# Reordering the first batch of a fused attention and MLP kernel, and handing one rearrangement to GpSimd

## The chip, the cores and the metric

The kernel runs on one core of one Trainium2 chip. The core has a matrix engine (TensorE, "PE" in the profile), three engines for elementwise work (VectorE "DVE", ScalarE "ACT" and GpSimd "POOL"), and a queue engine (SyncE, "SP") that only issues transfers here. Each engine runs its own instructions strictly in order, and waits on semaphores for the results of others. The metric is the device time of one execution in microseconds (us), as the median of several runs.

## The reference, cut to what matters

```
# q, k, v: (8, 12, 448, 64); w_in: (768, 2048); w_out: (2048, 768); alpha: (2048,)
scores = (1/8) * q @ k^T                       # per batch and head, 448 x 448
attn   = relu(scores) ** 2 / 448
x      = (attn @ v), heads side by side        # (3584, 768)
h      = x @ w_in
g      = max(h, 0) + alpha * min(h, 0)
out    = g @ w_out                             # (3584, 768), float32
```

Eight batches of twelve heads go through attention; then all 3584 tokens go through two matrix products with a leaky relu, whose slope is given per column, between them.

## The kernel before, in words

**Tiles.** Heads are taken four at a time. Such a group is called a quad; a batch has three (`NG = 3`), so there are 24, numbered `n = 0..23`, and batch 0 is quads 0, 1 and 2. The 448 positions of a sequence are split as 64 x 7, and the seven residues `j = 0..6` are the "chunks" of a quad. All matrix inputs are bf16; q, k, v and the weights are cast on the way in by transfers that GpSimd issues (`load_qk`, `load_v`, `load_w_in`, `load_w_out`). At most eight of these are in flight: each issue waits for the landing of the one eight places before it. For quad 0 alone, q and half of k come in as float32 by other queues (L129) and are cast on the chip (L138 to L140).

**Attention of a quad.** First q and k are turned, so that the head dimension lies on the partitions. There are two ways: `turn_pe` (L149) transposes on TensorE and copies the result out of PSUM into a tile `T`; `turn_dma` (L161) has VectorE rearrange q and k into a tile `perm` by two copies (L164), and then a transposing transfer on SyncE's queue writes `T`. Quads 0 to 4 are turned on TensorE, the rest by transfer. For each chunk, `score_mm` (L173) makes four matmuls into a pair of PSUM banks, `relu` (L184) takes them out as bf16 into one of seven `rl` buffers, on ScalarE (L187) or VectorE (L189), and `square` (L192) squares that into one of twelve `at` buffers. `attnv` (L200), called A@V here, multiplies the seven squared chunks with v in 28 matmuls, and two copies scale the result into `xT` (L215 to L218).

**The MLP.** `f1` (L254) makes six matmuls for one block of 128 hidden columns (`km` = 0, 1 need quad 0 of the batch, 2, 3 quad 1, and 4, 5 quad 2), and `f1_out` applies the leaky relu with one ScalarE and one VectorE instruction (L249, L250) into `gT`. Two batches share a `gT`; `f2` (L259) multiplies it with w_out, whose columns are held in two parts, the first third and the rest.

**What sets the order.** `tc.manual_schedule()` is on, so each engine's order is that of the program text. The text is a long list written out by hand: `sc(...)` makes scores and relus for given chunks and puts them on the list `late`; `sq(k)` squares the oldest `k` of that list; loads and turns stand between them. PSUM banks are given out by `take_bank`, `take_pair` and `hold` to whoever asks, the least recently taken first, and a taker waits until the earlier user's result has been read out. `some_early` lets f1 of batch 0 start on `km` 0 to 3 of its first four blocks, in four banks that are held, before A@V of quad 2 is done. From batch 1 on, attention chunks of the next batch are spread between f1 and f2.

**Around the change.** Batch 0 has no earlier work to fill TensorE with, so its chunks follow each other through score, relu and square. In front of quad 5's chunks stands a gate: `landed` (L376), a GpSimd copy of one element of quad 5's `T`, which holds back all loads behind it in GpSimd's queue until the transposing transfer of quad 5 has landed.

Of the kernel before, what the change touches and what calls it, by code (L numbers as in the profile page):

```python
# [13 lines left out]
ALU = mybir.AluOpType  # L14

PP = 64
NJ = 7
# [3 lines left out]
def kernel(  # L21
# [10 lines left out]
    nc = tc.nc  # L32
    B, H, S, D = q.shape
# [27 lines left out]
    alpha_sb = singles.tile([128, KF], F32)  # L61
    beta_sb = singles.tile([128, KF], F32)
    landed = singles.tile([1, 1], BF16)
# [28 lines left out]
    raw, vraw = {}, {}  # L92

    def load_qk(n, names="qk"):
        b, g = divmod(n, NG)
        for name in names:
            src = q if name == "q" else k
            t = raw_pool.tile([128, 2, NJ, D], BF16, tag=name, name=f"{name}raw")
            flat = src[b].rearrange("(m two) (pp j) d -> (two pp) m (j d)", two=2, j=NJ)
            nc.gpsimd.dma_start(out=t.rearrange("p m j d -> p m (j d)"), in_=flat[:, 2 * g:2 * g + 2])  # L100
            raw[(n, name)] = t

    def load_v(n):
        b, g = divmod(n, NG)
        t = v_pool.tile([128, 2, NJ, D], BF16, tag="v", name="vraw")
        flat = v[b].rearrange("(m two) (pp j) d -> (two pp) m (j d)", two=2, j=NJ)
        nc.gpsimd.dma_start(out=t.rearrange("p m j d -> p m (j d)"), in_=flat[:, 2 * g:2 * g + 2])  # L107
        vraw[n] = t
# [4 lines left out]
    def load_w_in(i):  # L113
        lo, hi = 512 * i, 512 * i + 512
        for hf in range(2):
            for e in range(2):
                nc.gpsimd.dma_start(out=w_in_sb[64 * hf:64 * hf + 64, :, e, lo:hi],  # L117
                                    in_=w_in_v[hf, e, :, :, lo:hi])

    def load_w_out(h, lo=0, hi=KF, step=4):  # L120
        for lo in range(lo, hi, step):
            nc.gpsimd.dma_start(out=w_out_sb[h][:, lo:lo + step], in_=w_out_v[:, lo:lo + step, COLS[h][0]:COLS[h][1]])

    FIRST = 4
    first, flat0 = {}, {}
# [9 lines left out]
    warm = psum[:, 7, :128]  # L135
    for _ in range(36):
        nc.tensor.matmul(warm, ident, ident, start=True, stop=True)
    for name, lo, hi, copy in (("q", 0, 4, nc.vector.tensor_copy), ("q", 4, NJ, nc.scalar.copy),  # L138
                               ("k", 0, 2, nc.vector.tensor_copy), ("k", 2, FIRST, nc.scalar.copy)):
        copy(raw[(0, name)][:, :, lo:hi].rearrange("p m j d -> p m (j d)"), first[name][:, :, D * lo:D * hi])  # L140
    load_qk(1)
    load_v(0)
    load_qk(2)
# [3 lines left out]
    T = {}  # L147

    def turn_pe(n, parts=(("q", 0, NJ, "D"), ("k", 0, NJ, "D"))):  # L149
        if n not in T:  # L150
            T[n] = T_pool.tile([128, 2, NJ, 128], BF16, tag="T", name="T")
        for name, lo, hi, eng in parts:
            ps = take_bank().bitcast(BF16)
            for j in range(lo, hi):
                for s in range(2):
                    nc.tensor.transpose(ps[64 * s:64 * s + 64, 128 * j:128 * j + 128], raw[(n, name)][:, s, j], ident)  # L156
            dst = T[n][:, "qk".index(name), lo:hi].rearrange("p j c -> p (j c)")
            copy = nc.vector.tensor_copy if eng == "D" else nc.scalar.copy
            copy(dst, ps[:, 128 * lo:128 * hi])  # L159

    def turn_dma(n):  # L161
        p = perm_pool.tile([128, 2, NJ, 2, D], BF16, tag="perm", name="perm")
        for i, name in enumerate("qk"):
            nc.vector.tensor_copy(p[:, i], raw.pop((n, name)).rearrange("p s j d -> p j s d"))  # L164
        t = T_pool.tile([128, 2, NJ, 128], BF16, tag="T", name="T")
        nc.sync.dma_start_transpose(out=t.rearrange("p a j c -> p (a j) c"),
                                    in_=p.rearrange("p a j s d -> p (a j s d)"))
        T[n] = t
# [23 lines left out]
    def square(n, j, rl, eng="D"):  # L192
        a = at_pool.tile([128, 2, S], BF16, tag="at", name="at")
        if eng == "A":
            nc.scalar.activation(a, rl, ACTF.Square)
        else:
            nc.vector.tensor_tensor(a, rl, rl, ALU.mult)  # L197
        att[(n, j)] = a

    def attnv(n):  # L200
        ps = take_pair()
        vv = vraw.pop(n)
        for j in range(NJ):
            a = att.pop((n, j))
            for r in range(2):
                for s in range(2):
                    nc.tensor.matmul(ps[64 * s:64 * s + 64, r, :S],  # L207
                                     vv[64 * r:64 * r + 64, s, j, :],
                                     a[64 * r:64 * r + 64, s],
                                     start=(j == 0), stop=(j == NJ - 1))  # L210
        b, g = divmod(n, NG)
        if g == 0:
            xT[b] = xT_pool.tile([128, NG, 2, S], BF16, tag="xT", name="xT")
        if n == 0:
            nc.scalar.activation(xT[b][:, g], ps[:, :, :S], ACTF.Copy, scale=out_scale)  # L215
            return
        nc.scalar.activation(xT[b][:, g, 0], ps[:, 0, :S], ACTF.Copy, scale=out_scale)  # L217
        nc.vector.tensor_scalar(xT[b][:, g, 1], ps[:, 1, :S], out_scale, None, ALU.mult)  # L218

    late = []  # L220

    def sc(chunks):

        for n, j, eng in chunks:
            late.append((n, j, relu(score_mm(n, j), eng)))

    def sq(k=99, eng="D"):
        for g in late[:k]:
            square(*g, eng)
        del late[:k]  # L230
# [28 lines left out]
    def f2(sb, c, h, parts=None):  # L259

        first_col, width = COLS[h][0], COLS[h][1] - COLS[h][0]
        o = o_pool.tile([128, d_model - CUT], F32, tag="o", name="osb")
        for lo, hi in parts or ((0, width),):
            ps = take_bank()[:, :hi - lo]
            for ff in range(KF):
                nc.tensor.matmul(ps, gT[sb][:, ff, bass.ts(c, 128)], w_out_sb[h][:, ff, lo:hi],  # L266
                                 start=(ff == 0), stop=(ff == KF - 1))
            nc.scalar.copy(o[:, lo:hi], ps)  # L268
            for u in range(2):
                blk = 2 * c + u  # L270
                b, j = 2 * sb + blk // NJ, blk % NJ
                rows = out[b * S:(b + 1) * S].rearrange("(pp j) d -> j pp d", j=NJ)
                eng = nc.scalar if u and parts else nc.sync
                eng.dma_start(out=rows[j][:, first_col + lo:first_col + hi], in_=o[64 * u:64 * u + 64, lo:hi])  # L274
# [4 lines left out]
    def ch(n, lo, hi, p=pat):  # L279
        return [(n, j, p[j]) for j in range(lo, hi)]  # L280

    load_w_in(0)
    load_v(2)
    load_w_in(1)
    turn_pe(0, (("q", 0, 4, "D"), ("q", 4, NJ, "A"), ("k", 0, 2, "D"), ("k", 2, FIRST, "D")))
    sc(ch(0, 0, 3))
    turn_pe(0, (("k", FIRST, NJ, "D"),))
    sc(ch(0, 3, 4))
    sq(3)
    load_qk(3)  # L290
    sc(ch(0, 4, 6))
    turn_pe(1)
    sc(ch(0, 6, 7))
    sq(4)
    load_w_in(2)
    load_w_in(3)
    sc(ch(1, 0, 3, "AAA"))
    attnv(0)
    load_qk(4)
    sq(2)  # L300
    sc(ch(1, 3, 4))
    turn_pe(2)
    sq(1)
    sc([(1, 4, "D"), (1, 5, "A"), (1, 6, "A")])
    sq(2)
    load_w_out(0, 0, 8)
    load_qk(5)
    load_v(3)
    load_w_out(0, 8)
    early = {}  # L310
    todo = []

    def some_early(count):
        for ff, km in todo[:count]:
            if ff not in early:
                early[ff] = hold()
            f1_mm(psum[:, early[ff], :S], 0, ff, (km,))
        del todo[:count]

    sc(ch(2, 0, 3, "AAA"))  # L320
    sq(3)
    attnv(1)
    load_v(4)
    load_v(5)
    todo = [(ff, km) for ff in range(4) for km in range(4)]
    sc(ch(2, 3, 5, "AAAAAAA"))
    sq(2)
    some_early(4)
    sc(ch(2, 5, 7, "AAAAADA"))
    some_early(8)  # L330
    square(*late.pop(-2), "A")
    sq()
    attnv(2)
    nc.vector.tensor_scalar(beta_sb, alpha_sb, -1.0, 1.0, ALU.mult, ALU.add)
    some_early(4)
    for ff in range(4):
        f1_mm(psum[:, early[ff], :S], 0, ff, range(4, KM))
        f1_out(psum[:, early[ff], :S], 0, ff)
# [14 lines left out]
            turn_dma(n)  # L353
        load(n + 2)

    turn_pe(3)
    f1s(0, 4, 6)
    sc(ch(3, 0, 3))
    f1s(0, 6, 8)
# [11 lines left out]
    del late[:]  # L371
    f1s(0, 13, 16)
    late += kept
    load_qk(6)
    load_qk(7, "q")
    nc.gpsimd.tensor_copy(landed, T[5][:1, 0, 0, :1])  # L376
    load_qk(7, "k")
    load_qk(8)
    load_w_out(1)
    load_v(6)  # L380
    f2(0, 0, 0)
# [4 lines left out]
    sq(3)  # L386
    sq(2, "A")
    sq()
    turn_dma(6)
    load_qk(9)  # L390
    load_v(7)
    load_v(8)
    load_v(9)
    f2(0, 1, 0)
    f2(0, 2, 0)
    sc(ch(5, 0, 3))
    sq(1)
    attnv(4)
# [61 lines left out]
    for b in range(2, B):  # L460
# [15 lines left out]
        for i, u in enumerate(units):  # L476
            if i in at and not last:
                g = at[i]
# [37 lines left out]
```

## Time and profile before

| | |
|---|---|
| device time, median of 3 runs | 386.19 us (385.89 to 386.44) |
| span of the profiled execution | 384.3 us |
| busy: PE, DVE, ACT, POOL | 374.4, 266.4, 206.8, 67.9 us |
| DMA | 43.42 MB, mean 113 GB/s |
| costliest groups | f2 matmuls (L266) 149.8 us, f1 matmuls (L241) 149.9 us, relus on ScalarE (L187) 97.9 us, squares on VectorE (L197) 91.6 us |

Busy times of different engines overlap, so they don't add up to the span. What tells which engine sets the end is the chain: followed backwards from the last instruction, at each step to what released it. A long busy time of an engine off that chain costs nothing. Matmuls are pipelined, so that a matmul's own length (about 350 ns here) is more than its share of TensorE's time; the steps between starts count, about 190 ns for 448 columns. The view of waits gives for each engine the idle time and who ended it, and the table of stretches shows in which part of the run an engine is full.

### The profile page before, as it was taken

The numbers are of one execution on the slowest core, as the hardware profiler recorded it, in microseconds if no ns is written. First come the engines' busy times: TensorE is split into PE (matmuls) and PEld (weight loads), VectorE is DVE, ScalarE is ACT, GpSimd is POOL, SyncE is SP. The second block draws the span as 40 slices with busy tenths as digits, with TensorE's granted clock in tenths as the row PEclk, the third lists the DMA queues.
The fourth block names the chain that finished last, engine by engine and source line by source line (L and its number), as shares of the span: only waits on it lengthen the run. The fifth ranks groups of instructions, "written<-read, shape, count | busy, mean of one in ns | idle before, by whom it ended". The sixth has DMA issues, their size and how long they took to land.

```text
span 384.3 us, 7838 instructions
## 1 busy us (share of the span) xinstructions
PE 374.4 (97%) x3178; PEld 204.9 (53%) x3200; DVE 266.4 (69%) x422; ACT 206.8 (54%) x331; POOL 67.9 (18%) x102
## 2 busy tenths in 40 slices
PE   7799999999999999999999999999999999999996
PEld 5444564545554455555465555544556445645554
DVE  4987987775777988688656887779855788526300
ACT  5977687546463654465444656547544475434321
POOL 8556235132202202022200222020000000000000
PEclk9999999999999999999999999999999999999999
DMA  9999999999993666688292872946036300120023
GB/s 161 187 203 202 201 124 208 184 194 235 178 183 56 112 116 104 113 135 119 47 165 60 136 122 47 170 73 123 15 84 89 77 0 16 43 68 2 14 68 84
DMA packets 73284, 43.42 MB, mean 113 GB/s; under 512 B 40352, under 2 KB 69792, under 8 KB 73248
## 3 DMA queue, kind: packets, MB, share of 16 engines
q0 software_dynamic: 26864, 22.45, 39.1%
q1 hardware_dynamic: 45952, 20.07, 27.2%
q8 instruction: 25, 0.41, 0.4%
q10 hardware_dynamic: 432, 0.39, 0.3%
q14 instruction: 11, 0.09, 0.1%
HBM read 45.62 MB, written 11.01 MB: 147 GB/s over the span
## 4 chain that ended last, share of the span: by engine, by line
PE 92%; DMA 4%; DVE 3%; issue 0%; ACT 0%; ACTq 0%
PE psum L241 38%; PE psum L266 37%; PE psum L178 9%; PE psum L207 8%; DMA T<-perm 3%; DVE at L197 2%; DMA qfirst<-in_q_dram 1%; PE psum L156 1%; DVE T L159 1%; DVE rl L189 1%; ACT osb L268 0%; ACTq L274 0%; DVE qraw L140 0%
## 5 line engine op out<-in xcount | busy, mean ns | idle before, releaser
L266 PE MATMUL psum<-w_out,gT 128*128 128x256 bf16 (+3 forms) x890 | 149.8, 322 | 1.2
L241 PE MATMUL psum<-xT,w_in_sb 128*128 128x448 bf16 x768 | 149.9, 353 | 0.0
L266 PEld LDWEIGHTS <-gT 128*128 128x128 bf16 x912 | 86.6, 98 | 64.4 <-issue 8.2
L241 PEld LDWEIGHTS <-w_in_sb 128*128 128x128 bf16 x768 | 73.4, 98 | 73.1 <-issue 5.9
L250 DVE SCALAR_TENSOR_TENSOR gT<-neg,beta_sb,psum 128x448 bf16<-128x448 f32 x128 | 83.5, 677 | 35.6 <-ACT neg L249 35.5
L249 ACT ACTIVATE neg<-psum 128x448 f32<-128x448 f32 x128 | 69.2, 546 | 61.2 <-PE psum L241 59.4
L187 ACT ACTIVATE rl<-psum 128x896 bf16<-128x896 f32 x113 | 97.9, 931 | 1.9 <-PE psum L178 1.9
L197 DVE TENSOR_TENSOR at<-rl 128x896 bf16<-128x896 bf16 x164 | 91.6, 618 | 0.0
L189 DVE TENSOR_SCALAR rl<-psum 128x896 bf16<-128x896 f32 x55 | 59.7, 1086 | 39.6 <-PE psum L178 39.5
L268 ACT COPY osb<-psum 128x256 f32<-128x256 f32 (+3 forms) x57 | 26.9, 473 | 104.5 <-PE psum L266 98.7
L178 PE MATMUL psum<-T 64*64 64x448 bf16 x672 | 44.7, 356 | 3.2 <-DVE T L159 1.4
L100 POOL DMA_DIRECT2D qraw<-in_q_dram x23 | 16.6, 721 | 156.9 <-DVE perm L164 148.1
L207 PE MATMUL psum<-at,vraw 64*64 64x448 bf16 x672 | 36.6, 350 | 0.3 <-DVE at L197 0.2
L178 PEld LDWEIGHTS <-T 64*64 64x64 bf16 x672 | 16.5, 106 | 21.8 <-issue 12.5
L207 PEld LDWEIGHTS <-vraw 64*64 64x64 bf16 x672 | 21.0, 107 | 12.6 <-issue 2.3
L218 DVE TENSOR_SCALAR xT<-psum 128x448 bf16<-128x448 f32 x23 | 14.4, 625 | 14.5 <-PE psum L207 10.9
L107 POOL DMA_DIRECT2D vraw<-in_v_dram x24 | 17.5, 729 | 7.2 <-DMA w_out<-in_moe_w_out_dram 4.2
L100 POOL DMA_DIRECT2D kraw<-in_k_dram x23 | 16.6, 722 | 6.9 <-DVE gT L250 3.7
L217 ACT ACTIVATE xT<-psum 128x448 bf16<-128x448 f32 x23 | 12.6, 549 | 2.6 <-PE psum L207 2.6
L164 DVE COPY perm<-qraw 128x896 bf16<-128x896 bf16 x19 | 11.6, 612 | 0.0
L164 DVE COPY perm<-kraw 128x896 bf16<-128x896 bf16 x19 | 11.6, 609 | 0.0
L117 POOL DMA_DIRECT2D w_in_sb<-in_moe_w_in_dram x16 | 10.0, 633 | 6.5 <-DMA vraw<-in_v_dram 2.2
(25 smaller groups left out, 40.3 us busy)
## 6 DMA issues: line engine op xcount, KB each, us to landing
out_dram<-osb SPq DMA_DIRECT2D x54, 128.0 KB, 2.4
vraw<-in_v_dram POOLq DMA_DIRECT2D x24, 224.0 KB, 8.4
qraw<-in_q_dram POOLq DMA_DIRECT2D x23, 224.0 KB, 5.3
kraw<-in_k_dram POOLq DMA_DIRECT2D x23, 224.0 KB, 6.9
out_dram<-osb SPq DMA_DIRECT2D x56, 64.0 KB, 2.2
w_in_sb<-in_moe_w_in_dram POOLq DMA_DIRECT2D x16, 192.0 KB, 8.5
w_out<-in_moe_w_out_dram POOLq DMA_DIRECT2D x4, 512.0 KB, 12.8
w_out<-in_moe_w_out_dram POOLq DMA_DIRECT2D x4, 256.0 KB, 8.9
```

What stands on the lines that cost most here:

```text
L100: nc.gpsimd.dma_start(out=t.rearrange("p m j d -> p m (j d)"), in_=flat[:, 2 * g:2 * g + 2])
L164: nc.vector.tensor_copy(p[:, i], raw.pop((n, name)).rearrange("p s j d -> p j s d"))
L178: nc.tensor.matmul(ps[64 * c:64 * c + 64, r, :S], t[64 * r:64 * r + 64, 1, j, 64 * c:64 * c + 64], t[64 * r:64 * r + 64, 0, :, 64 * c:64 * ...
L187: nc.scalar.activation(rl, ps[:, :, :S], ACTF.Relu)
L189: nc.vector.tensor_scalar(rl, ps[:, :, :S], 0.0, None, ALU.max)
L197: nc.vector.tensor_tensor(a, rl, rl, ALU.mult)
L207: nc.tensor.matmul(ps[64 * s:64 * s + 64, r, :S], vv[64 * r:64 * r + 64, s, j, :], a[64 * r:64 * r + 64, s], start=(j == 0), stop=(j == NJ ...
L241: nc.tensor.matmul(ps, w_in_sb[:, km // 2, km % 2, bass.ts(ff, 128)], xT[b][:, km // 2, km % 2, :], start=(km == 0), stop=(km == KM - 1))
L249: nc.scalar.activation(neg, ps, ACTF.Relu, scale=-1.0)
L250: nc.vector.scalar_tensor_tensor(gT[b // 2][:, ff, (b % 2) * S:(b % 2) * S + S], neg, beta_sb[:, ff:ff + 1], ps, ALU.mult, ALU.add)
L266: nc.tensor.matmul(ps, gT[sb][:, ff, bass.ts(c, 128)], w_out_sb[h][:, ff, lo:hi], start=(ff == 0), stop=(ff == KF - 1))
L268: nc.scalar.copy(o[:, lo:hi], ps)
```

## The change

It has three parts, all in the first 60 us.

- *Quad 0 in small pieces.* q and k of quad 0 are cast in seven pieces instead of four, turned in nine groups instead of five, and the pieces are shared out between VectorE and ScalarE. The aim is that the first scores start earlier.
- *Batch 0 in a new order.* The list of scores, relus, squares and A@V is rewritten, with each square named by its chunk (`sq_of`). More squares and turn copies go to ScalarE and one more relu to VectorE. A@V of quads 0 and 1 come later, and all sixteen early f1 matmuls are in front of A@V of quad 2. Quad 3 is turned directly behind that A@V instead of after f1's first four blocks. The loads of quad 3 go ahead of the later quarters of w_in.
- *Quad 6 by GpSimd.* The gate on quad 5's transfer moves in front of the loads of quads 6 and 7. The two rearranging copies of quad 6 move from VectorE to GpSimd, right behind the loads, and its transposing transfer is issued after two f2 units instead of before them.

The amount of work is the same: the same matmuls, relus, squares and bytes. The diff, cut to its core:

```diff
-    def turn_dma(n):
+    def rearrange_rows(n, eng):
         p = perm_pool.tile([128, 2, NJ, 2, D], BF16, tag="perm", name="perm")
         for i, name in enumerate("qk"):
-            nc.vector.tensor_copy(p[:, i], raw.pop((n, name)).rearrange("p s j d -> p j s d"))
+            eng.tensor_copy(p[:, i], raw.pop((n, name)).rearrange("p s j d -> p j s d"))
+        return p
+
+    def turn_dma(n, p=None):
+        p = p or rearrange_rows(n, nc.vector)
...
-    for name, lo, hi, copy in (("q", 0, 4, nc.vector.tensor_copy), ("q", 4, NJ, nc.scalar.copy),
-                               ("k", 0, 2, nc.vector.tensor_copy), ("k", 2, FIRST, nc.scalar.copy)):
...
-    turn_pe(0, (("q", 0, 4, "D"), ("q", 4, NJ, "A"), ("k", 0, 2, "D"), ("k", 2, FIRST, "D")))
-    sc(ch(0, 0, 3))
-    turn_pe(0, (("k", FIRST, NJ, "D"),))
-    sc(ch(0, 3, 4))
-    sq(3)
-    load_qk(3)
-    sc(ch(0, 4, 6))
-    turn_pe(1)
-    sc(ch(0, 6, 7))
-    sq(4)
-    load_w_in(2)
-    load_w_in(3)
-    sc(ch(1, 0, 3, "AAA"))
-    attnv(0)
...
+    cast0("q", 0, 2, "D")
+    cast0("q", 5, 7, "A")
+    cast0("q", 4, 5, "A")
+    cast0("q", 3, 4, "D")
+    cast0("q", 2, 3, "D")
+    cast0("k", 1, 4, "D")
+    cast0("k", 0, 1, "A")
+    turn_pe(0, (("q", 0, 2, "D"),))
+    turn_pe(0, (("q", 3, 4, "A"),))
...
+    turn_pe(0, (("k", 3, 4, "A"),))
+    sc([(0, 0, "A")])
+    sc([(0, 1, "D")])
+    sc([(0, 2, "A")])
+    turn_pe(0, (("k", 4, 7, "D"),))
+    load_qk(3)
+    load_w_in(1)
+    load_w_in(2)
+    load_w_in(3)
+    sq_of(0, 0, "D")
+    sc([(0, 3, "A")])
+    turn_pe(1, (("q", 0, 7, "D"),))
...
+    sq_of(1, 4, "D")
+    sq_of(1, 6, "D")
+    sc([(2, 1, "A")])
+    attnv(0, "AD")
+    sc([(2, 2, "A")])
+    nc.vector.tensor_scalar(beta_sb, alpha_sb, -1.0, 1.0, ALU.mult, ALU.add)
+    attnv(1, "AD")
+    sc([(2, 3, "A")])
+    sq_of(2, 0, "A")
+    sc([(2, 4, "D")])
+    sq_of(2, 4, "A")
+    sq_of(2, 1, "D")
+    some_early(5)
+    some_early(4)
+    sq_of(2, 2, "D")
+    sq_of(2, 3, "D")
+    sc([(2, 5, "A")])
+    sq_of(2, 5, "A")
+    sc([(2, 6, "D")])
+    some_early(7)
+    sq_of(2, 6, "D")
+    attnv(2, "AD")
+    turn_pe(3, (("k", 0, 7, "D"),))
+    turn_pe(3, (("q", 0, 7, "D"),))
...
-    turn_pe(3)
...
+    nc.gpsimd.tensor_copy(landed, T[5][:1, 0, 0, :1])
     load_qk(6)
-    load_qk(7, "q")
-    nc.gpsimd.tensor_copy(landed, T[5][:1, 0, 0, :1])
-    load_qk(7, "k")
+    load_qk(7)
     load_qk(8)
+    rows6 = rearrange_rows(6, nc.gpsimd)
     load_w_out(1)
...
-    turn_dma(6)
...
     f2(0, 1, 0)
     f2(0, 2, 0)
+    turn_dma(6, rows6)
```

## The prediction

> **What bounds the kernel now.** I read the page's chain first: who holds the end of the program?
>
> ```profile
> PE 374.4 (97%) x3178; PEld 204.9 (53%) x3200; DVE 266.4 (69%) x422; ACT 206.8 (54%) x331; POOL 67.9 (18%) x102
> ...
> PE 92%; DMA 4%; DVE 3%; issue 0%; ACT 0%; ACTq 0%
> ```
>
> TensorE is the chain for 92% of the span, and the change removes no matmul. Time can come only out of its waits, so I looked for them with the table of stretches (columns: stretch, its length, busy us of PE, PEld, DVE, ACT, POOL with counts, granted clock, DMA share, GB/s).
>
> ```profile
> 8.00:10.00 2.00, 1.62 (x38) 1.09 (x39) 2.00 (x5) 2.00 (x4) 1.14 (x2) 1.00 1.23 188
> 10.00:12.00 2.00, 1.12 (x26) 0.55 (x21) 2.00 (x5) 2.00 (x4) 1.06 (x2) 1.00 1.26 201
> ...
> 16.00:18.00 2.00, 1.14 (x20) 0.63 (x23) 2.00 (x4) 2.00 (x4) 0.89 (x2) 1.00 1.18 181
> ...
> 20.00:25.00 5.00, 5.00 (x57) 2.15 (x50) 4.37 (x8) 3.92 (x6) 2.51 (x4) 1.00 1.25 203
> ...
> 50.00:55.00 5.00, 4.72 (x65) 3.57 (x67) 4.41 (x7) 4.12 (x7) 1.12 (x3) 1.00 0.83 111
> ```
>
> Until 20 us ScalarE and VectorE are busy all the time and TensorE is not; from 20 us TensorE is full, but for 0.28 us in 50 to 55. DMA moves about 200 GB/s all the while up to 50 us. The timeline shows the places that matter (start, length, engine, line, what, and the idle time in front of it).
>
> ```profile
> 7.16 7.39 ACT L187 ACTIVATE rl<-psum 128x896 bf16<-128x896 f32 x9 [0.60 <-PE psum L178]
> ...
> 23.45 1.52 PE L207 MATMUL psum<-at,vraw 64*64 64x448 bf16 x28
> ...
> 24.91 2.44 PE L241 MATMUL psum<-xT,w_in_sb 128*128 128x448 bf16 x12
> ...
> 37.03 0.70 POOL L107 DMA_DIRECT2D vraw<-in_v_dram  x1 [0.45 <-DMA kraw<-in_k_dram]
> 37.05 0.45 PEld L156 LDWEIGHTS <-kraw 128*64 128x64 bf16 x14
> ...
> 43.45 5.15 SPq L166 DMA_TRANSPOSE T<-perm  x1
> ...
> 53.41 0.76 PE L178 MATMUL psum<-T 64*64 64x448 bf16 x12 [0.28 <-DMA T<-perm]
> ```
>
> Three readings. ScalarE runs nine relus in 7.2 us, 0.80 each, without a hole: it paces batch 0. The k of quad 4 landed just before 37.03 (the trace has 36.75), and TensorE turns it at 37.05: that load has only 0.3 us to spare. And the only wait of TensorE after 20 us that can be named is for the transposing DMA of quad 5: issued at 43.45, landed at 53.37, 9.9 us, where the transposes of the whole run have a median of 6.4 us from issue to landing.
>
> **What the Trainium skill says.** "DMA: Bandwidth & Descriptors", section Queues, rings and completion order: each DMA engine takes turns between the queues that have work for it, packet by packet. The trace agrees: the quad 5 transposes took 9.9 us with q and k of quad 6 and q of quad 7 in flight beside them, against 6.4. "SBUF — State Buffer", section SBUF: two separate sides: a VectorE instruction with two SBUF inputs and a GpSimd one that reads SBUF take a shared port in turn, each for its whole length. No run here shows it. "TensorE: Matmul & The Clock Gate", section What's actually happening: an idle window of about 3.4 us halves the clock. The granted clock of before stays 1.00 through all of batch 0, with TensorE at 1.12 of 2 us in the emptiest stretches.
>
> **The change, part by part.**
>
> *Quad 0 in small pieces.* Seven casts and nine copies replace four and five. A VectorE copy out of PSUM took 0.286 us at 256 elements and 0.425 at 512, so about 0.22 at 128; a ScalarE one 0.479 at 384, 0.27 at 128 on the same slope of 0.83 ns an element. Laid in order from the landing of q at 4.91: the last copy that chunk (0,0) needs ends near 6.49, the scores start at 6.54 for 6.72 before, and the first relu at about 6.97 for 7.16. That is 0.19 us.
>
> *Batch 0 in a new order.* ScalarE still paces it, so I laid out its queue. Relus are 0.80 apart (nine in 7.2; the same rule puts the first xT of before at 7.16 + 7.2 = 14.36, measured 14.35), squares 0.85 (two of them: 50.58 to 51.43), half an xT 0.45. After: nine relus from 6.97 to 14.17; 0.2 until the square of (0,4) on VectorE, which runs back to back from 7.15 at 1.0 a relu and 0.54 a square or full copy, frees a relu buffer; two relus to 15.97; the copy of k 5 to 7 of quad 2, 0.30; three relus to 18.67; xT 0.45; a relu; xT; a relu to 21.17; two squares to about 22.8; the relu of (2,5) ends at 23.8. A@V of quad 2 takes the bank pair that this relu frees, so it starts at 23.85, its last two squares being done at 24.4 and 24.8 when their matmuls come up, and ends at 25.2. Before it started at 23.45 and gave way at 24.91, but with 12 of the 16 early matmuls of f1 done; all 16 are done now, which is 4 x 0.198 = 0.79 us of matmul less behind it. Equal work stands at 25.7 before and 25.2 after: 0.5 us gained. I allow 0.4 either way, since about 60 steps are chained. The 13th and 14th squares wait for the A@V of quad 0 to give buffers back; that runs from 16.4, those squares come up at 17.9 and 18.4, so nothing waits.
>
> *Quad 3 turned behind A@V of quad 2.* 28 transposes, 0.90 us, in both kernels. They now lie where TensorE would wait for the xT copies (0.6 us) of that A@V; before, four early matmuls filled that hole. No net change. Its loads now go ahead of the second quarter of w_in: k of quad 3 near 22.4, needed at 25.2; that quarter near 26.5, needed at 27.7. Hidden.
>
> *The limit on what is gained.* All loads up to k of quad 4 are the same bytes on the same full queue, so k still lands near 36.75. TensorE, 0.5 us earlier, wants it at 36.55. So at most 0.3 us gets past this point; the rest becomes a wait. I count 0.33 for the first three parts.
>
> *The landed gate earlier, quad 6 by GpSimd.* q and k of quad 6 and q of quad 7 no longer load beside the quad 5 transposes: those had 4.6 us more company before (until 52.3; after, v of quad 5 at 47.7 is the last). I put their landing at 50, between 49.5 (issued at 43.1, 6.4 us alone) and 52 (most of the present delay kept). TensorE comes at 53.13 - 0.33 = 52.8. The 0.28 us go. VectorE loses two copies of 0.61 at 52.4, when TensorE doesn't wait for it: nothing. On GpSimd no trace has such a copy; "GPSIMD Engine Reference", section Elementwise — side-by-side cycle accounting, states 1.03 cycles an element as the floor and 2.6 for two inputs, so an estimate of 896 x 1.03 / 1.2 GHz = 0.77 us, up to 1.94. I take 1.1. Six issues of 0.71 from 50.2 end at 54.5, two copies at 56.7 (58.4 at the worst), and only then the second half of w_out, queued behind them, is issued: 56.19 before. Its last piece landed at 76.03, and is wanted about 81 (16 matmuls of 512 columns from 78.7). It may slip to 78: hidden. T of quad 6 is issued near 57 for 53.6, lands by 66, and is wanted at 78: hidden. The port shared with VectorE can hold a square for one GpSimd copy, about 1 us, in a stretch where no A@V is within 2 us of its squares.
>
> *Sum.* 0.33 + 0.28 = 0.61: 386.19 - 0.61 = 385.6.
>
> **The rivals.**
>
> (1) The loads are not the limit: a changed order lets k of quad 4 land some 0.5 us earlier. Then all of 0.5 us, or 0.9 at the good end of my layout, comes through: 0.28 + 0.5 to 0.9, about 385.0. For it: the queue runs at 171 to 182 GB/s in parts of 12 to 18 us. Against: eight loads are always outstanding, and the rate is flat at 203 from 20 us.
>
> (2) Batch 0 gains nothing, since one more hole of 0.5 us opens on ScalarE, which has two squares and four copies more than before for one relu less; only the transposes' wait goes: 385.9.
>
> (3) Slower, by batch 0. A@V of quads 0 and 1 now come at 16.4 and 18.2 for 12.2 and 17.9; between 9.4 and 12.8 TensorE has only four chunks and a turn, about 35% of the time. If the clock is halved there, or one relu waits on one square in the chain of seven buffers, A@V of quad 2 comes 1.5 us late, less the 0.28: 387.4. Against: my longest hole is 1 us.
>
> (4) Slower, by GpSimd: copies of several us, or held by VectorE, push the second half of w_out past 82; TensorE waits about 1.5 us: 387.1.
>
> **How the numbers follow.** The layout as summed 0.50, rival 1 0.17, rival 2 0.15, rival 3 0.12, rival 4 0.06. Faster by over 0.2% means under 385.4: rival 1 and two fifths of the main case, 0.38. Slower over 387.0: rivals 3 and 4, 0.18. The rest, 0.44, is within 0.2%. The range runs from 384.8, past rival 1, to 387.0, where it leaves most of rivals 3 and 4 out.
>
> **What would show it.** In the profile after: the first relu near 7.0; A@V of quad 2 near 23.9 with all sixteen early matmuls ahead of it; a wait of 0.1 to 0.3 us of TensorE for k of quad 4 near 36.8; no wait for T at 52.8, its landing near 50; GpSimd copies near 1.1 us; w_out landed by 78. It is wrong if A@V of quad 2 comes after 24.5, if k of quad 4 lands off 36.75 by over 0.5, if a new wait stands after 53 us, or if the clock row falls under 9 in its first slices.

## The result

The changed kernel takes 388.12 us (median of 4 runs, 387.61 to 388.21) against 386.27 us (4 runs, 385.89 to 386.44) before: a ratio of 1.0046, 95% interval 1.0029 to 1.0064. It is slower by 1.8 us, where 385.6 was forecast. Ratios leave disturbed runs out, so a few below differ from what two medians give.

The profiled span grew from 384.28 to 386.33 us. First the page of the changed kernel: busy times, and the chain by engine.

```profile
PE 375.9 (97%) x3178; PEld 206.3 (53%) x3200; DVE 266.4 (69%) x423; ACT 208.2 (54%) x337; POOL 69.7 (18%) x104
...
PE 83%; DMA 8%; issue 4%; ACT 2%; DVE 1%; POOL 1%; ACTq 0%; POOLq 0%; DVEq 0%
```

TensorE fell from 92% to 83% of the chain, and DMA rose from 4% to 8%. The table of stretches, in the columns used before, says where TensorE is no longer full.

```profile
16.00:18.00 2.00, 1.68 (x40) 1.14 (x40) 2.00 (x5) 2.00 (x5) 1.01 (x3) 1.00 1.22 190
20.00:25.00 5.00, 5.00 (x52) 2.21 (x46) 4.95 (x9) 4.97 (x7) 2.89 (x5) 1.00 1.24 202
50.00:55.00 5.00, 5.00 (x70) 3.90 (x71) 3.70 (x6) 4.43 (x7) 4.70 (x8) 1.00 0.76 86
55.00:60.00 5.00, 4.53 (x44) 1.74 (x36) 5.00 (x8) 3.34 (x5) 3.77 (x5) 1.00 1.07 177
75.00:80.00 5.00, 4.19 (x33) 2.48 (x35) 4.10 (x7) 1.30 (x3) 1.60 (x3) 1.00 1.23 193
```

The 0.28 us hole of 50 to 55 is closed, as forecast. Two new ones stand after it: 0.47 us in 55 to 60 and 0.81 us in 75 to 80. Before, the last two stretches read:

```profile
55.00:60.00 5.00, 5.00 (x56) 2.16 (x52) 4.93 (x9) 3.94 (x6) 4.88 (x7) 1.00 1.26 134
75.00:80.00 5.00, 4.95 (x41) 2.93 (x41) 3.08 (x5) 3.00 (x5) 1.43 (x2) 1.00 1.24 193
```

The timeline of the changed kernel shows both holes, with the marks that the prediction named.

```profile
7.33 0.92 ACT L188 ACTIVATE rl<-psum 128x896 bf16<-128x896 f32 x1 [0.33 <-PE psum L179]
...
24.15 1.52 PE L208 MATMUL psum<-at,vraw 64*64 64x448 bf16 x28
...
36.53 0.58 PE L153 MATMUL psum<-ident,qraw 128*64 128x128 bf16 x14
37.19 0.58 PE L153 MATMUL psum<-ident,kraw 128*64 128x128 bf16 x14
...
53.15 0.76 PE L179 MATMUL psum<-T 64*64 64x448 bf16 x12
...
54.72 0.97 POOL L161 COPY perm<-qraw 128x896 bf16<-128x896 bf16 x1
54.86 1.32 DVE L198 TENSOR_TENSOR at<-rl 128x896 bf16<-128x896 bf16 x1
...
56.10 0.61 DVE L219 TENSOR_SCALAR xT<-psum 128x448 bf16<-128x448 f32 x1
...
56.76 1.10 PE L242 MATMUL psum<-xT,w_in_sb 128*128 128x448 bf16 x5 [0.47 <-DVE xT L219]
...
75.31 0.62 DVE L161 COPY perm<-qraw 128x896 bf16<-128x896 bf16 x1 [3.02 <-DMA T<-perm]
...
78.28 0.10 PEld L267 LDWEIGHTS <-gT 128*128 128x128 bf16 x1 [0.47 <-DVE gT L251]
```

*The first hole.* A square took 1.32 us instead of 0.62, beside GpSimd's copy of quad 6's q. Behind it on VectorE stood half the xT copy of A@V of quad 4, and TensorE's f1 waited for that. The same square before:

```profile
55.12 0.61 DVE L197 TENSOR_TENSOR at<-rl 128x896 bf16<-128x896 bf16 x1
```

*The second hole.* VectorE stood still for 3.02 us in front of its rearranging copies of quad 8, and the `gT` operations behind them came late for f2. What VectorE waited for is named in brackets: a transposing transfer. There are two perm buffers, so quad 8 writes the one that quad 6 used, and may do so only when quad 6's transfer has read it. The pieces of the chain say how long that took (start, length, what).

```profile
57.87 17.32 DMA T<-perm
76.46 1.89 DVE gT L251 x4
```

Quad 6's transfer ran 17.3 us, from 57.87 to 75.19. Before, it was issued at 53.59 and landed at 60.66: 7.1 us.

TensorE's own marks give the account: quad 5's first scores start 0.26 us earlier than before (53.15 for 53.41), f1 of batch 1 is 0.37 later at 61.37, quad 6's first scores 1.71 later (79.69 for 77.98), and that stays up to TensorE's last end (382.41 for 380.71). So: -0.26 for the transfer of quad 5, +0.63 at 56, +1.34 at 78. (The profile's brackets show less, 0.47 and 0.81, since they count only from the end of the matmul in front; the starts show what was lost.) From TensorE's end to the end of the span 0.35 us more passed than before (3.92 for 3.57). Over all profiles of this document that tail has two values: 3.9 to 4.1 us in the six in which GpSimd rearranges quad 6 and w_out follows at once, and 3.55 to 3.57 in the other eleven. So it seems to belong to the quad 6 part too; why is open.

### The profile page after: what moved, and what is told of

Read it like the earlier page. It is cut to its first block, busy times and chain, and to the rows that moved or that the text cites. A ratio compares the mean times of both kernels' runs of the same rounds, so it can differ in the third digit from the quotient of the medians.

```text
span 386.3 us, 7848 instructions
## 1 busy us (share of the span) xinstructions
PE 375.9 (97%) x3178; PEld 206.3 (53%) x3200; DVE 266.4 (69%) x423; ACT 208.2 (54%) x337; POOL 69.7 (18%) x104
## 4 chain that ended last, share of the span: by engine, by line
PE 83%; DMA 8%; issue 4%; ACT 2%; DVE 1%; POOL 1%; ACTq 0%; POOLq 0%; DVEq 0%
PE psum L267 36%; PE psum L242 30%; PE psum L179 8%; PE psum L208 7%; DMA T<-perm 4%; DMA w_out<-in_moe_w_out_dram 2%; ACT rl L188 2%; DMA kraw<-in_k_dram 1%; PE psum L137 1%; PE psum L153 1%; DVE gT L251 1%; DVE perm L161 0%; POOL perm L161 0%; ACT osb L269 0%; POOL kraw L100 0%
## 5 line engine op out<-in xcount | busy, mean ns | idle before, releaser
L190 DVE TENSOR_SCALAR rl<-psum 128x896 bf16<-128x896 f32 x56 | 60.8, 1086 | 40.5 <-PE psum L179 40.3
L218 ACT ACTIVATE xT<-psum 128x448 bf16<-128x448 f32 x24 | 13.4, 559 | 2.3 <-PE psum L208 2.3
```

Of the source, the lines that this page charges most:

```text
L190: nc.vector.tensor_scalar(rl, ps[:, :, :S], 0.0, None, ALU.max)
```

## The experiments

### Which part of the change costs: quad 6 undone, and quad 6 alone

The theory was that the quad 6 part makes all of the loss; the rival, that batch 0 does.

```diff
 # quad 6 undone: the changed kernel, except
-    nc.gpsimd.tensor_copy(landed, T[5][:1, 0, 0, :1])
     load_qk(6)
-    load_qk(7)
+    load_qk(7, "q")
+    nc.gpsimd.tensor_copy(landed, T[5][:1, 0, 0, :1])
+    load_qk(7, "k")
     load_qk(8)
-    rows6 = rearrange_rows(6, nc.gpsimd)
...
+    turn_dma(6)
     load_qk(9)
...
-    turn_dma(6, rows6)
```

"Quad 6 alone" is the kernel before with just these lines the other way round.

> The changed kernel with the quad 6 part undone: gate, loads, VectorE rearrangement and transfer of quad 6 as before; quad 0 in pieces and the new order of batch 0 kept. Theory A (all the loss is in the quad 6 part: 0.6 us where GpSimd's copies hold a square, 1.3 us where VectorE waits for a perm buffer): no gain from batch 0 either, since k of quad 4 lands at 37.1 and the wait for quad 5's T stays, so 386.1 to 386.4, against 386.27 before. Rival B (the new batch 0 costs time itself): 387 or more.

> The kernel before with only the quad 6 part of the change: gate ahead of the loads of quads 6 and 7, the two copies on GpSimd, the transfer issued after two f2 units. Theory A: the whole loss, 386.27 - 0.3 (no wait for quad 5's T) + 0.6 + 1.3 = 387.9 to 388.2. Rival B (batch 0 costs the time): 386.0 to 386.4.

Quad 6 undone: 386.04 us, ratio 1.0002 [0.9993, 1.0010]. Quad 6 alone: 387.97 us, 1.0043 [1.0031, 1.0055]. The quad 6 part makes the whole loss, and batch 0 neither gains nor loses at the end. The second one's profile has VectorE's wait of the second hole again, and its scores of quad 6 start 0.96 us later than before. The first hole is missing there: no square was held, and GpSimd's second copy took 1.14 us instead of 0.93. At 387.51 us it is also one of the quicker of the five runs.

```profile
74.57 0.62 DVE L164 COPY perm<-qraw 128x896 bf16<-128x896 bf16 x1 [2.83 <-DMA T<-perm]
...
78.14 0.28 PE L270 MATMUL psum<-w_out,gT 128*128 128x256 bf16 x1 [0.31 <-DVE gT L254]
78.73 0.28 PE L270 MATMUL psum<-w_out,gT 128*128 128x256 bf16 x1 [0.31 <-DVE gT L254]
```

### The waiter: a third perm buffer, and VectorE instead of GpSimd

```diff
-    perm_pool = ctx.enter_context(tc.tile_pool(name="perm", bufs=2))
+    perm_pool = ctx.enter_context(tc.tile_pool(name="perm", bufs=3))
```

The second kernel has this too, and VectorE does quad 6's copies after the scores of quad 5's chunks 3 and 4.

> The changed kernel with three perm buffers instead of two, so that VectorE's copies of quad 8 don't wait for quad 6's transposes. Theory A: the wait of 3 us on VectorE at 72 us and the 1.3 us of TensorE behind it go: 388.12 - 1.3 = 386.8. Rival C (TensorE would wait there anyway, for the second half of w_out or for T of quads 6 and 7, which land just as late): 387.8 to 388.2.

> The changed kernel with three perm buffers, and with quad 6 rearranged by VectorE after the squares that follow quad 4's A@V, when its k has landed, instead of by GpSimd. Theory A (a GpSimd copy holds back a square on VectorE, and TensorE waits 0.6 us behind it at 56 us): 386.8 - 0.6 = 386.2. Rival D (the 0.6 us come from something else there, or VectorE's two copies cost as much): 386.7 to 387.

Three buffers: 386.40 us, 1.0004 [0.9998, 1.0011] (22 runs, one of them of 723.98 us). The transfer of quad 6 is as slow as ever (56.67 to 74.51), VectorE doesn't wait, and TensorE has no hole at 78:

```profile
55.00:60.00 5.00, 5.00 (x52) 2.10 (x48) 4.80 (x8) 3.82 (x6) 4.40 (x7) 1.00 1.18 201
75.00:80.00 5.00, 4.95 (x41) 2.92 (x41) 3.08 (x6) 3.14 (x5) 1.81 (x3) 1.00 1.24 194
```

So it was the buffer, not the scores of quad 6, that the late transfer held up. The medians differ by 1.7 us, of which 1.34 are the second hole. The first hole is missing in this profile as well, though the third buffer comes into use only with quad 7's copies at 65 us: that part is a matter of phase, as shown below. TensorE ends 0.21 us earlier than before here, and the tail behind it is 0.49 longer.

VectorE instead: 386.15 us, 1.0002 [0.9994, 1.0009], not told apart from three buffers alone. Its profile is of a run slower than that median, 386.66 us. No square is held, but the two copies, 0.53 apart, now stand in front of the last square of A@V of quad 5; and as quad 6's transfer is issued later still (60.05 to 77.72), quad 8's, issued at 78.13 behind it, lands at 99.01, when TensorE already wants it. Against the profile of three buffers alone, some 0.55 us is lost at each of two other places (the lead over its marks goes from 0.26 us to -0.28 at the first and on to -0.83 at the second):

```profile
60.57 0.57 PE L208 MATMUL psum<-at,vraw 64*64 64x448 bf16 x8 [0.35 <-DVE at L198]
...
99.06 0.76 PE L179 MATMUL psum<-T 64*64 64x448 bf16 x12 [0.47 <-DMA T<-perm]
```

### Why the transfer took 17 us: w_out held back until it had landed

```diff
-    load_w_out(1)
-    load_v(6)
     f2(0, 0, 0)
...
+    f2(0, 1, 0)
+    f2(0, 2, 0)
+    turn_dma(6, rows6)
+    nc.gpsimd.tensor_copy(landed, T[6][:1, 0, 0, :1])
+    load_w_out(1)
+    load_v(6)
     load_qk(9)
...
-    f2(0, 1, 0)
-    f2(0, 2, 0)
-    turn_dma(6, rows6)
```

> The changed kernel, with two perm buffers, and a second gate: the second part of w_out and all loads behind it are issued only when the transposes of quad 6 have landed. Theory A (those transposes take 17 us only because w_out's loads run beside them): they land in 6 to 7 us, near 64, VectorE no longer waits at 72, and TensorE waits for the last pieces of w_out instead, which land near 77 to 80: 386.8 to 388. Rival E (they take 17 us for another reason, such as the out transfers ahead of them in the same queue): they land near 75 again, w_out after 85, and TensorE waits 5 us: 392 or more.

The transfer went from 57.48 to 64.09, in 6.6 us, as quick as quad 5's in the changed kernel (43.29 to 49.90, also 6.6). The times from issue to landing of the transfers of quads 6, 7 and 8 (least, median, most), first in the changed kernel and then in this one:

```profile
DMA to landing us min/median/max: 17.3/20.0/20.5
...
DMA to landing us min/median/max: 6.6/17.4/19.9
```

With two perm buffers still, VectorE no longer waits in front of quad 8's copies, and TensorE has no hole at 78: the other end of the same cause. So it is the second part of w_out, with the loads queued behind it, that makes the transfer slow. The head start over w_out's first issue goes with it: 2.6 us ahead before, 7.1 us; 1.9 ahead with quad 6 undone, 8.2; issued within 0.1 us of w_out's first piece in the changed kernel, 17.3. It is not all that counts. In the three kernels further down with the gate between quads 6 and 7 the transfer had 2.2 to 2.3 us of head start and took 10.4 to 12.1 us; q of quad 7 loads there behind the gate, one load more beside the transfer than before, but what made the difference was not tested.

This kernel takes 387.46 us (1.0035 [1.0022, 1.0048]), so it brings nothing. In its profile (386.77 us) GpSimd's copy holds a square to 1.74 us, for a step of 1.25 us between two matmuls at 55.4, and TensorE waits 0.30 us for a later transfer at 107. w_out lands at 81.0 there, without a wait; whether the slower runs wait for it isn't known.

### GpSimd's copies and VectorE's squares: the copies made twice

```diff
-            eng.tensor_copy(p[:, i], raw.pop((n, name)).rearrange("p s j d -> p j s d"))
+            for _ in range(2 if eng is nc.gpsimd else 1):
+                eng.tensor_copy(p[:, i], raw[(n, name)].rearrange("p s j d -> p j s d"))
+            raw.pop((n, name))
```

> This is the version with three perm buffers, with each of GpSimd's two copies of quad 6 made twice in a row (the second writes the same values again; the output is the reference's). Theory A (the port: a square on VectorE with two inputs in SBUF is held until the GpSimd copy that runs at the time has ended): four GpSimd copies of about 0.95 us, so twice as many squares are held, each ending some 0.48 us after a GpSimd copy's end, and twice the chance that an A@V or f1 matmul of TensorE waits behind one: 386.4 for three buffers alone, plus 0.3 to 0.9, so about 386.9. Theory B (no port; the copies only take GpSimd's time, and the second part of w_out, queued behind them, is 2 us later): 386.4, and the squares beside the copies keep their 0.62 us.

387.01 us, 1.0017 [1.0009, 1.0024], against 1.0003 [0.9994, 1.0011] for three buffers with quad 4's load moved, which ran beside it; the two intervals just overlap, so the times alone are an indication. The squares say more. Three were held, to 1.00, 0.72 and 1.34 us. One by one, the holds end at the same distance from the copy's end: a GpSimd copy ends at 54.82, the square at 55.31 (0.49 later); 57.01 and 57.48 (0.47); 58.28 and 58.75 (0.47). In the changed kernel it is 55.68 and 56.17 (0.49), 57.84 and 58.32 (0.48); with three buffers 55.10 and 55.59 (0.49). A square that starts free takes 0.62. All ten held squares of six profiles end 0.47 to 0.49 us after a copy. That is what a lock held to the copy's end looks like: the Trainium skill, "SBUF — State Buffer", section SBUF: two separate sides, says as much, and here it shows. It works the other way round too: GpSimd's copies that met a square took 1.14 to 1.22 us instead of 0.93 to 0.98. By that section the instruction that starts first has the port; the recorded starts don't always show it, since with w_out held back the held square's record starts 0.31 us ahead of the copy's (54.28 and 54.59).

How much a hold costs depends on a few tenths of phase: with three buffers the square was held to 0.81 us and TensorE waited for nothing; with quad 4's load moved it was held to 1.38 and TensorE waited 0.53.

### What the small pieces give

Three perm buffers, and quad 0 as before:

```diff
-    cast0("q", 0, 2, "D")
...
-    turn_pe(0, (("k", 3, 4, "A"),))
+    turn_pe(0, (("q", 0, 4, "D"), ("q", 4, NJ, "A"), ("k", 0, 2, "D"), ("k", 2, FIRST, "D")))
```

> Three perm buffers, with quad 0 cast, turned and copied in the large pieces of before; the new order of batch 0 and the rest of the change stay. Prediction as made: the small pieces bring the first relu 0.19 us earlier, and the load of quad 4's k then takes most of it as a wait of TensorE near 36.9, so 386.4 to 386.5. Rival: the small pieces are worth nothing or lose, 386.2 to 386.4, since after k of quad 4 the start no longer shows. Told apart less by the time than by the first relu (near 7.2 for 7.05) and by TensorE's start on k of quad 4.

386.73 us, 1.0016 [1.0009, 1.0023], some 0.4 us worse than the 1.0003 and 1.0004 with small pieces, with intervals that just overlap. In its profile the first relu is at 7.46 and A@V of quad 2 at 24.26. That profile alone cannot size the pieces, though, since the first relu goes with the time at which TensorE's clock came up, which varied from 4.2 to 7.3 us between profiles of all versions. Where q had landed by 4.95 us and the clock came late (after 6.7), old pieces give 7.45 and 7.46, small ones 7.32 to 7.34; with an early clock (by 4.8) 7.16 and 7.03 to 7.06. So they give 0.10 to 0.14 us. Where the rest of the 0.4 comes from isn't shown: the profile, of a run of 387.22 us, has a wait of 0.32 us for k of quad 4 and one of 0.58 for the port, both of which come and go between profiles.

### What keeps batch 0's lead from coming through

*Quad 4's load first* (three buffers):

```diff
     load_w_in(1)
     load_w_in(2)
-    load_w_in(3)
...
     load_qk(4)
+    load_w_in(3)
```

> Three perm buffers, with the load of quad 4 ahead of the last quarter of w_in. If the landing of k of quad 4 near 36.9 is what keeps batch 0's gain from coming through, that wait goes (TensorE turns q near 36.2 and k 0.4 later) and up to 0.4 us comes through: 386.0. If the gain is given back at the next load or the next wait, 386.4 as with three buffers alone.

386.42 us, 1.0003 [0.9994, 1.0011]. The landing of k can hold TensorE: with the load in its old place TensorE waited for it in four profiles of this batch 0, up to 0.47 us, and in others it came in time. Now k lands at 33.08, quad 4 is turned without a wait, 0.47 us earlier than before (36.23 for 36.70), and so is everything up to 55.4. There the held square takes 0.53 back. Not a gain, but the lead was real.

*The gate between quads 6 and 7*, with batch 0 old, new, and new with quad 4's load first. This keeps quad 5's transfer free of one load, and quad 6 on VectorE in its old place:

```diff
     load_qk(6)
-    load_qk(7, "q")
     nc.gpsimd.tensor_copy(landed, T[5][:1, 0, 0, :1])
-    load_qk(7, "k")
+    load_qk(7)
```

> The kernel before with one line moved: the gate on quad 5's T stands between the loads of quad 6 and those of quad 7. Quad 6 is still rearranged by VectorE at its old place. Theory A: q of quad 7 no longer runs beside the transposes of quad 5, which land near 51.5 instead of 53.4, so the 0.28 us wait goes and nothing else moves: 386.0 against 386.2. Rival: those transposes are slow by themselves, and still land near 53: 386.2.

> The same move of the gate, on the changed kernel with the quad 6 part otherwise undone: quad 0 in pieces and the new order of batch 0 kept. Theory A (batch 0 gains up to 0.5 us, and the landing of k of quad 4 takes all but 0.1 to 0.3 of it): 385.8 to 386.0. Rival (the load is not the limit): 385.5.

> The kernel of the run before this one with one load moved: q and k of quad 4 are loaded ahead of the last quarter of w_in. Theory A: k of quad 4 lands near 33, so TensorE no longer waits for it near 37, and all that batch 0 gains (0.1 to 0.5 us, with the time at which the clock comes up) gets through: 385.5 to 385.7, the fastest of all. Rival: no gain in batch 0 to let through: as the run before it.

388.40 us (385.68 to 392.72), 386.83 (385.56 to 389.78) and 386.54 (385.19 to 389.03); ratios 1.0052 [1.0029, 1.0076], 1.0023 [1.0009, 1.0037] and 1.0019 [1.0003, 1.0034]. The best runs beat before and the rest lose. In the three profiles w_out's last piece lands at 82.5, 81.7 and 79.3, right when f2 comes to it, and TensorE waits 0.80, 0.41 and 0 us for it; that the slower runs lose by the same wait is likely, not shown. The first profile:

```profile
82.49 0.81 PE L266 MATMUL psum<-w_out,gT 128*128 128x512 bf16 x3 [0.80 <-DMA w_out<-in_moe_w_out_dram]
```

In the profile of the third TensorE waits for nothing after 20 us, and its last matmul ends at 380.03, for 380.71 before: there the lead did come through, in a run of 385.35 us.

*Quad 5's load earlier too*, with the quad 6 part undone:

```diff
-    f1s(0, 10, 12)
-    sc(ch(3, 6, 7) + ch(4, 0, 2, "AA"))
+    f1s(0, 10, 11)
     turn_dma(5)
+    f1s(0, 11, 12)
+    sc(ch(3, 6, 7) + ch(4, 0, 2, "AA"))
```

and `load_qk(5)` ahead of the first load of w_out, `load_qk(4)` ahead of `load_w_in(3)`.

> The change without its quad 6 part, with the loads of quads 4 and 5 each ahead of the weight quarter or part in front of them, and quad 5 rearranged one f1 unit earlier. Quad 4's k lands near 33 and quad 5's k near 40, the transposing transfer of quad 5 is issued near 42 and lands before 52; both waits (k of quad 4, T of quad 5) go without touching the gate, and the second part of w_out is issued no later than before, so that it doesn't land at the edge. Theory: 0.5 to 0.8 us faster than before, about 385.5, with little scatter. Rival: the transposing transfer still takes 9 to 10 us beside the loads and the scores of quad 5, which now come at 52.6, wait for it: 386.0.

387.01 us, 1.0025 [1.0009, 1.0041]: a miss. The transfer was issued at 41.86 and landed at 54.25, 12.4 us; it now ran beside the last 3.4 us of w_out's first part (before, 2.0), which may be the reason; that was not tested. TensorE waited 0.57 us for it, and the copies moved on VectorE kept f1's `gT` from TensorE for 0.88 us at 42.4. An earlier issue bought a later landing.

*w_out ahead of quad 8's loads*, gate as above, quad 8 rearranged after quad 6's first scores; batch 0 old, and new with quad 4's load first:

```diff
-    load_qk(8)
     load_w_out(1)
     load_v(6)
+    load_qk(8)
...
     run(some(3))
+    turn_dma(8)
```

> The kernel before with the gate between the loads of quad 6 and quad 7, the second part of w_out issued ahead of quad 8's q and k, and quad 8 rearranged after the first scores of quad 6. The second part of w_out lands some 3 us earlier than with the gate moved alone, so near 79 for 82.5, and no longer at the edge; the wait for quad 5's transposes (0.28) goes. Theory (the lead of the new batch 0 is real and only later waits eat it): this one gains the 0.28 alone, about 385.8, with little scatter. Rival (a wait for quad 8's transposes takes its place): 386.3 or more.

> The same moves of gate, w_out and quad 8 with the change's batch 0, and quad 4's load ahead of the last quarter of w_in; quad 6 is rearranged by VectorE as before. Theory: the waits for k of quad 4, quad 5's transposes and w_out are all gone, so the lead of 0.8 us that the best profile showed comes through in every run: 385.3, some 0.5 less than with the old batch 0. Rival (batch 0 is worth nothing at the end): the same time as with the old batch 0.

The times scatter from 385.85 to 399.01 (median 391.98) and from 385.26 to 399.73 (389.33), so neither is of use; the intervals are [1.0008, 1.0061] and [0.9996, 1.0045]. Their lowest runs answer the question in part: five of 14 with the old batch 0 at 385.85 to 386.42, four of 14 with the new at 385.26 to 385.38. They are picked from the low end, so this is an indication, not a measurement. The profiled run of the second, of 397.49 us, shows a DMA that moves 59 and 94 GB/s at a busy share of 1.34 and 1.49, in two stretches in which the profiled run of the first moves 195 and 196 GB/s:

```profile
60.00:64.00 4.00, 4.00 (x35) 2.03 (x28) 2.12 (x4) 2.77 (x7) 0.72 (x1) 1.00 1.34 59
64.00:68.00 4.00, 4.00 (x23) 2.08 (x22) 4.00 (x8) 2.06 (x5) 0.00 (x0) 1.00 1.49 94
```

w_out then lands at 82.8 and quad 8's transposes keep TensorE 3.7 us. In both profiles quad 6's transfer runs beside w_out and takes 17 us; why the rate falls in only some runs is open.

*Quad 4's load first, gate and quad 6 as before*, which moves nothing behind quad 4:

> The change without its quad 6 part (gate, loads and rearranging of quad 6 as before), with the load of quad 4 ahead of the last quarter of w_in. TensorE turns quad 4 near 36.2 and 36.65 without a wait. The transposing transfer of quad 5 is issued 0.4 us earlier than before with the same company, so it lands near 53.0, when TensorE wants it at 52.6: a wait of about 0.4 us, and 0.4 us of the lead come through: 385.7 to 385.8. Rival (the lead is not time, or is lost to another wait behind quad 5): 386.1 to 386.3.

386.14 us, 1.0004 [0.9995, 1.0014]. The rival holds, in the time. Quad 5's transfer, issued at 43.41, landed at 53.60, and TensorE waited for it, twice as long as before:

```profile
53.65 0.57 PE L179 MATMUL psum<-T 64*64 64x448 bf16 x8 [0.55 <-DMA T<-perm]
```

With loads of quads 6 and 7 beside it the transfer took 10.2 us, so what lead batch 0 has up to there can end as a wait for it. In this profile the lead was also small (36.66 for 36.70 at quad 4), for a reason that the clock shows:

```profile
14.00:16.00 2.00, 2.00 (x26) 1.01 (x25) 2.00 (x5) 2.00 (x3) 1.34 (x3) 0.50 1.18 182
16.00:18.00 2.00, 2.00 (x32) 0.96 (x32) 2.00 (x5) 2.00 (x4) 0.75 (x2) 0.65 1.15 182
```

TensorE's clock was halved from 14.00 to 17.41 us. That is rival 3's mechanism, at a fraction of its price. No version beat before by its interval.

## Why the prediction was wrong

*The step that failed* is this one: "T of quad 6 is issued near 57 for 53.6, lands by 66, and is wanted at 78: hidden." The issue was right (57.87). The rest failed twice.

- The length. It landed at 75.19, since it was issued together with the second part of w_out; without w_out and the loads behind it it takes 6.6 us, with them 17.3 (shown by holding them back). The prediction allowed about 9 us. It had read that a transfer slows beside loads for quad 5, where it cost 3.5 us, and gave quad 6 about as much, though its head start of 2.6 us over w_out was gone. The numbers were in the trace of before: the two transfers that followed there, beside w_out and the loads behind it, took 16.3 us (65.31 to 81.63) and 18.9 (73.04 to 91.91). The median of 6.4 over the run had hidden them; the same line (least, median, most over the run) had the 18.9 in it:

```profile
DMA to landing us min/median/max: 4.0/6.4/18.9
```

- The waiter. "Wanted at 78" looked at the scores that read `T`. The first to want the landing was the next writer of the transfer's source: VectorE's copies for quad 8 at 72.3, as `perm` has two buffers. A third buffer closes that hole, 1.34 us of TensorE's time, with the transfer as slow as ever, and a quick transfer closes it with two buffers (both shown).

*The port.* The prediction had a square held by one GpSimd copy, "in a stretch where no A@V is within 2 us of its squares". The hold was right: 0.7 us on one square, 0.07 on the other. The place was wrong. A@V of quad 4 runs at 53.74, and VectorE's queue held half of its xT copy right behind the held square; TensorE lost 0.63 us in all. What counted was not the square's own reader but what stood behind it on VectorE. Whether it costs anything is a matter of phase: in four of the seven profiles with GpSimd's copies TensorE lost 0.5 us or more there, in the others 0.3 or nothing.

*What was right.*

- Quad 5's transfer: landing forecast 50, measured 49.90; TensorE's wait of 0.28 us went, and quad 5's scores came 0.26 us earlier.
- GpSimd: copies forecast at 1.1 us, measured 0.97 and 0.93; w_out landed by 76.8 (forecast 78), hidden.
- Batch 0: A@V of quad 2 forecast at 23.85, measured 24.15. In the seven profiles of this batch 0 with small pieces whose clock came up between 4.1 and 5.6 us and whose q had landed by 4.95 it was 23.83 to 23.87, and quad 4 was turned 0.46 to 0.49 us earlier than before, for 0.5 forecast. In the changed kernel's profile the clock came up only at 7.32 us, against 4.50 in that of before, and the lead at quad 4's q was 0.17.
- Small pieces: 0.10 to 0.14 us for 0.19; the mechanism held and the term was too large.
- k of quad 4: landed at 37.14, forecast 36.75; TensorE's start on it 0.66 us after q instead of 0.41, so a wait of 0.25, within the 0.1 to 0.3 forecast. With the late clock, though, that wait was more than the lead: f1 behind it stood 0.10 us later than before (37.70 for 37.60), where 0.33 of gain was forecast. That k lands at a fixed time was too simple: with the same loads ahead of it, it landed from 36.25 to 37.49 in eight profiles, a spread wider than the lead.

*The rivals.* Rival 4 had the right part of the change and the right side, through the wrong wait: in the changed kernel w_out was never late. Rival 3's halved clock does happen with the new batch 0, in some runs, but quad 6 undone ties with before, so it isn't the loss. Rival 1 finds no support: k of quad 4 landed at 37.14, and its 36.25 to 37.49 over eight profiles is no earlier than the 36.30 to 37.64 of four with the old order. Rival 2 is right that batch 0 gains nothing in the end, but not by its hole on ScalarE, which is busy all through 8 to 20 us.

*The sum.* Forecast -0.33 - 0.28. In the changed kernel's profile TensorE stands at +0.10 behind quad 4 and at -0.26 at quad 5, with the wait there gone; then come +0.63 for the port and +1.34 for the perm buffer, which makes +1.71, and 0.35 of tail. Had the failed step cost nothing, three perm buffers show what would have been left: a tie. Of the four signs of being wrong that the prediction named, one came: a new wait after 53 us. (A slip in its chances: rival 1 and two fifths of the main case make 0.37, not 0.38.)

## What to carry to other kernels

Before you delay a transfer, look up what it will then run beside, and read its length from transfers that had that same company, not from a median over the run. List who waits for it at both ends: the reader of what it writes, and the next writer of what it reads, counted in buffers of the pool. And where GpSimd takes over a copy, look at what stands on VectorE behind an operation with two SBUF inputs, since that is what will be late.

## What the runs showed of the hardware

- A transposing transfer of one quad took 5.6 to 6.9 us with few loads beside it (quad 5 in the eight kernels that keep the loads of quads 6 and 7 behind it), and 17.3 issued together with 2 MB of w_out, in four loads, and the loads behind them. Issued first it was quicker: 2.6 us of head start gave 7.1 us, but 2.2 to 2.3 us gave 10.4 to 12.1 in three kernels with one load more beside it.
- GpSimd's rearranging copy of 128x896 bf16 took 0.93 to 0.98 us where no square was in its way, VectorE's 0.61.
- TensorE's clock halved in profiles of three versions with the new batch 0, at 14.06, 14.00 and 13.94 us, each 6.8 us after it had come up, for 3.4 us. No gap between two matmul starts from 7 to 16 us was longer than 1.04 us there; before had one of 1.25 and no halving. Between 10 and 14 us the records of these versions show 38 matmul starts, and those of before 50. The Trainium skill, "TensorE: Matmul & The Clock Gate", section What's actually happening, speaks of an idle window of about 3.4 us; the length agrees, but no such idle time was there, so a thinly filled window seems to be enough. It does not always do it: the changed kernel's profile has the same 38 and no halving. All three had the clock come up at 7.12 to 7.24 us; the nine profiles of this batch 0 where it came up before 7 us, and the changed kernel's at 7.32, had no halving, so where the thin stretch falls after that moment may decide. What share is needed was not tried.
- It does not seem to be rare: over eight variants with the new batch 0, without those in which the second part of w_out was held or landed late (and without the run of 723.98 us), the mean clock was under 0.997 in 35 of 122 runs, and in none of 188 runs of the kernel before. A halved clock for 3.4 of 384 us makes a mean of 0.996; where it fell is known for the profiled runs alone. In each of the eight the median of such runs lies above that of the others, by 0.2 to 0.6 us, with few runs each. So an estimate from these runs is that the new order of batch 0 has a price of some 0.3 us in about three runs of ten, which belongs on the other side of its lead of 0.47. How much of it is the halving, and how much the late coming up of the clock that went with it in the three profiles, was not separated.
